# Attention output as 32-row products per head, small copies moved to ScalarE, another list order, and the flag read earlier

## The chip, the cores and the metric

The kernel runs on one core of a Trainium2 chip. A core has five engines that run their own instruction streams beside each other: TensorE (PE, the matmuls; PEld is its weight load), VectorE (DVE), ScalarE (ACT), GpSimd (POOL) and SyncE (SP, which here only issues DMAs). The metric is the device time of one execution in microseconds (us), lower is better.

## The reference, cut to what matters

Three stages follow each other. An attention of 4 batches and 8 heads over 32 memory slots, a mixture of 8 experts with the two best per token, and a second MLP.

```python
def _attn_ref(q, k, v, phi):          # (4, 8, 576, 64), phi (4, 8, 576, 32)
    a = softmax(phi, over the 32 slots)
    k_m = np.einsum('bhsm,bhsd->bhmd', a, k)
    v_m = np.einsum('bhsm,bhsd->bhmd', a, v)
    attn = softmax(scale * q @ k_m.T)  # 576 x 32 per head
    return attn @ v_m                  # 576 x 64 per head

def _moe_ref(x, w_gate, w_noise, noise, w1, w2):   # x (2304, 512), 8 experts, F = 1024
    logits = x @ w_gate
    noisy = logits + log1p(exp(x @ w_noise)) * noise
    # two largest per token, softmax over them, relu(x @ w1[e]) @ w2[e], weighted sum

def _moe2_ref(x, w_in, w_out):         # 512 -> 2048 -> 512
    h = x @ w_in
    return (h * clip(h + 3, 0, 6) / 6) @ w_out
```

## The kernel before, in words

The attention is cut into 8 groups of four heads (batch b, half gi: g = 2b + gi). Four heads of 32 slots fill the 128 partitions. A group goes through the stages of the lists below: `ld` loads phi, q, k and v (L521 and on, queue SP); `a1` (L537) takes the softmax of phi; `q` (L553) transposes q on PE; `a2` (L571) multiplies it with k and v (72 products of 32x32 weights by 128 columns, L581) into km, scales them into kd (L585, L586), takes the largest value us of the v part (L594), and makes the transposed kT (L600, L602) and, with the gate's weights, a 16-column piece for the router's logits (L606, L609); `b` (L618) makes scores and their softmax `at`; `c` (L646) multiplies `at` with vb. vb (128 x 272) holds the four heads' v as a block diagonal of 256 columns, made by POOL (L649) from kd and the mask mp (L613), and the 16 logit columns. The product (L665) is taken in three pieces, each evacuated from PSUM by ACT (L667); after the second half of a batch DVE adds the logits (L671) and SP stores x to DRAM (L673).

After two batches the router (`route`, L682) finds the two best experts of each token and writes lists of token numbers, the first ones (ids0, L800) for an early part of expert 0, the full ones (ids, L802) at the end. POOL gathers rows of x by such a list (L836), PE transposes them (L853), and ACT and DVE split them into two fp16 parts (L855, L857). An expert's layer 1 is L870 (ACT L877, L878, DVE L880 follow), its layer 2 is L920, with ACT's yt (L923) and SP's store (L925) behind it. Weights come in as fp32 `st` (L447) and are split by ACT (L414) and DVE (L416). The second MLP (`ffn`, L994) runs over 6 chunks of 384 rows; its layer 1 is L1007, then DVE L1012, ACT L1014 (hf), DVE L1015, ACT L1017 (hh), DVE L1018; its layer 2 is L1031, and ACT L1045 and SP L1054 bring the rows out. `combine` (L931) gathers the two experts' rows of a chunk (ya and yb, L938), scales them (L945) and adds them. Last comes a flag: if the lists overflowed, a slower path runs behind `tc.If`; every engine loads the flag (L1226) and branches (L1227).

The order of the work is not that of the code. Functions register operations with an engine, a duration and dependences; `Sched` (L91) then places them on the engines by due times, in several rounds backwards and forwards, and each engine's instructions are written out in that order. It is steered by tables: `ORDER` and `W0`, `EAT` say in which step a group's stage is registered, `RUSH` shifts due times by stage and group, `W0G` says behind which group's loads the first expert's weights come. The operations fall into two segments; the first holds the attention, the router and the early part of expert 0, the second all the rest. Buffers are counted by tag: three of `kv`, so a load of group g + 3 waits for PE's products of group g.

## Time and profile before

| | |
|---|---|
| median of three runs | 917.58 us (917.4 to 918.63) |
| profiled execution | 916.52 us |
| its span | 914.7 us |
| instructions in the span | 16312 |
| PE busy | 874.2 us, 96% |
| DVE busy | 617.7 us, 68% |
| ACT busy | 436.9 us, 48% |
| POOL busy | 139.4 us, 15% |

Busy time is the time in which an engine executes at least one instruction; waiting, register work and DMA issues do not count. A line such as L665 is the source line that issued an instruction; a name such as kd is a tile, and `out<-in` says what is written from what. Idle time is put down to what ended it, so the table of shares is only the start: the waits and the chain of work have to be read stretch by stretch.

### The profile page before, as it was taken

What the parts mean: (1) busy time and instruction counts of PE and PEld (TensorE: products, weight loads), DVE (VectorE), ACT (ScalarE), POOL (GpSimd) and SP (SyncE); (2) the same over time, 40 slices, a digit from 0 to 9 for tenths busy, and PEclk for the clock granted to TensorE, in tenths of its full rate; (3) what the DMA queues carried; (4) which work ended last, traced back from release to release, by engine and by line L of the source; (5) the groups of instructions that cost most, each with busy time, mean ns of one, the idle gap of its engine ahead of it and who ended that gap; (6) DMA issues with size and microseconds to landing.
All of it is one profiled execution on the core that took longest, in us unless ns stands there. A gap on an engine that the chain in (4) does not pass through costs nothing.

```text
span 914.7 us, 16312 instructions
## 1 busy us (share of the span) xinstructions
PE 874.2 (96%) x6612; PEld 516.0 (56%) x6612; DVE 617.7 (68%) x1088; ACT 436.9 (48%) x665; POOL 139.4 (15%) x155
## 2 busy tenths in 40 slices
PE   6798699989999999999999998999999999999996
PEld 6676475654747565665656554555555555555552
DVE  6798965868697958688789896876464543333432
ACT  2386426665756647474836645453332422322222
POOL 2234211312021111000002123432010000000000
PEclk8999699999999999999999999999999999999998
DMA  9955335859996767959776546451310301200101
GB/s 342 362 173 179 95 127 198 284 166 224 214 262 211 214 216 200 229 123 282 238 231 213 171 145 177 105 139 52 78 35 1 78 1 18 52 1 2 33 1 38
DMA packets 109537, 135.14 MB, mean 148 GB/s; under 512 B 53008, under 2 KB 74000, under 8 KB 109456
## 3 DMA queue, kind: packets, MB, share of 16 engines
q1 hardware_dynamic: 103312, 114.63, 41.8%
q0 software_dynamic: 6144, 19.40, 8.0%
q8 instruction: 54, 0.88, 0.4%
q14 instruction: 27, 0.22, 0.1%
HBM read 94.74 MB, written 27.86 MB: 134 GB/s over the span
## 4 chain that ended last, share of the span: by engine, by line
PE 76%; DMA 4%; DVE 4%; issue 2%; ACT 1%; POOL 0%; SPq 0%; POOLq 0%; DVEq 0%; ACTq 0%
PE o L1031 19%; PE two L1007 18%; PE two L870 18%; PE o L920 14%; PE o L897 3%; DMA xg<-xf,ids 2%; PE da L870 1%; DMA ya<-ys,slot 1%; PE oa L920 1%; DMA st<-wf 1%; DVE yt L906 0%; DVE wam L457 0%; DVE xT L857 0%; DVE hh L880 0%; DVE xg L966 0%
## 5 line engine op out<-in xcount | busy, mean ns | idle before, releaser
L1031 PE MATMUL o<-wb,hh 128*128 128x512 f16 x864 | 194.8, 379 | 3.1 <-ACT hh L1017 2.4
L1007 PE MATMUL two<-xT,wa 128*128 128x384 f16 x1152 | 195.7, 326 | 0.0
L1007 PEld LDWEIGHTS <-wa 128*128 128x128 f16 x1152 | 112.5, 98 | 79.6 <-DVE wsm L400 0.2
L1031 PEld LDWEIGHTS <-hh 128*128 128x128 f16 x864 | 84.0, 98 | 99.7 <-ACT hh L1017 2.8
L920 PEld LDWEIGHTS <-hh 128*128 128x128 f16 x720 | 69.6, 98 | 80.5 <-issue 3.0
L1014 ACT ACTIVATE hf<-hf,c 128x768 f32<-128x768 f32 x48 | 44.9, 935 | 145.5 <-DVE hf L1012 138.7
L1012 DVE TENSOR_TENSOR hf<-two,ivb 128x768 f32<-128x768 f32 x48 | 45.9, 956 | 93.9 <-PE two L1007 93.8
L870 PE MATMUL two<-xT,wb 128*128 128x304 f16 (+2 forms) x768 | 103.8, 295 | 2.9 <-ACT hh L878 2.9
L870 PEld LDWEIGHTS <-wb 128*128 128x128 f16 x768 | 75.8, 99 | 31.0 <-issue 3.1
L870 PEld LDWEIGHTS <-wa 128*128 128x128 f16 x768 | 75.7, 99 | 29.9 <-issue 2.0
L870 PE MATMUL two<-xT,wa 128*128 128x304 f16 (+1 forms) x672 | 90.3, 295 | 0.7 <-DVE war L431 0.4
L920 PE MATMUL o<-wb,hh 128*128 128x512 f16 x384 | 86.5, 379 | 0.0
L920 PE MATMUL o<-wa,hh 128*128 128x512 f16 x336 | 75.3, 379 | 0.0
L880 DVE TENSOR_TENSOR hh<-hf,hh 128x608 f16<-128x608 f32 (+2 forms) x72 | 49.3, 689 | 37.8 <-ACT hh L878 35.6
L836 POOL DMA_INDIRECT xg<-xf,ids x40 | 46.3, 1157 | 161.6 <-DVE ya L845 57.4
L877 ACT ACTIVATE hf<-two 128x608 f32<-128x608 f32 (+2 forms) x72 | 42.9, 595 | 54.0 <-PE two L870 51.2
L1015 DVE SCALAR_TENSOR_TENSOR hh<-hf,two 128x768 f32<-128x768 f32 x48 | 45.7, 951 | 31.8 <-ACT hf L1014 31.6
L1018 DVE TENSOR_TENSOR hh<-hh,hh 128x768 f16<-128x768 f32 x48 | 45.9, 957 | 29.5 <-ACT hh L1017 29.5
L1017 ACT ACTIVATE hh<-hh 128x768 f16<-128x768 f32 x48 | 40.4, 842 | 41.8 <-DVE hh L1015 41.8
L416 DVE SCALAR_TENSOR_TENSOR wb<-st,wsm,wb 128x1024 f16<-128x1024 f32 x40 | 50.5, 1280 | 4.1 <-ACT wb L414 3.8
L416 DVE SCALAR_TENSOR_TENSOR wa<-st,wsm,wa 128x1024 f16<-128x1024 f32 x40 | 51.4, 1310 | 1.7 <-ACT wa L414 0.9
L414 ACT ACTIVATE wa<-st,wsm 128x1024 f16<-128x1024 f32 x40 | 44.1, 1144 | 8.1 <-DVE wsm L402 8.1
(220 smaller groups left out, 1079.7 us busy)
## 6 DMA issues: line engine op xcount, KB each, us to landing
st<-moe_w_d SPq DMA_DIRECT2D x32, 1024.0 KB
ys<-yt SPq DMA_DIRECT2D x32, 256.0 KB
w<-moe_w_in_d SPq DMA_DIRECT2D x16, 512.0 KB
wf<-w64o SPq DMA_DIRECT2D x32, 256.0 KB
w<-moe_w_out_d SPq DMA_DIRECT2D x16, 512.0 KB
st<-wf SPq DMA_DIRECT2D x8, 1024.0 KB
kv<-k_d SPq DMA_DIRECT2D x8, 576.0 KB
kv<-v_d SPq DMA_DIRECT2D x8, 576.0 KB
```

The source lines that it names most:

```text
L414: sch.op("ACT", act(1024, ptr=1), lambda s=s, w=w, c=c: ACT.activation(w.t[:, 0, c], s.t[:, c], AF.Copy, scale=sm.t[:, 2]), [(s, i), (sm, ...
L416: sch.op("DVE", 1.28, lambda s=s, w=w, c=c: DVE.scalar_tensor_tensor(w.t[:, 1, c], s.t[:, c], sm.t[:, 2], w.t[:, 0, c], op0=ALU.mult, op1= ...
L836: sch.op("POOL", 1.05, lambda t=t, xg=xg, tw=tw: POOL.indirect_dma_start(out=xg.t[:tw], out_offset=None, in_=xf[:rows], in_offset=bass.Ind ...
L870: PE.matmul(ph.t[:, i, :nw], wa.t[:, wi, c * 1024 + fb * 128:c * 1024 + fb * 128 + 128], xT.t[:, 4 * xi + c, o0 + i * nw:o0 + (i + 1) * nw ...
L880: sch.op("DVE", dve(n), lambda: DVE.tensor_tensor(hh.t[:, 1], hf.t, hh.t[:, 0], op=ALU.subtract), [hf, (hh, 0)], [(hh, 1)])
L920: PE.matmul(py.t[:tw], hs[fb].t[:, hi, tsl], wb.t[:, wi, fb * 512:(fb + 1) * 512], start=(fb == 0 and n == 0), stop=(fb == 7 and n == 2))
L1007: PE.matmul(ph.t[:, i, :CW], win[fb // 8].t[:, wi, o:o + 128], xT.t[:, 4 * xi + kc, :CW], start=(n == 0), stop=(n == 11))
L1012: sch.op("DVE", dve(768), lambda: DVE.tensor_tensor(t1.t, ph.t[:, :, :CW], ivb.t[:, None, :CW].to_broadcast([128, 2, CW]), op=ALU.mult), [ ...
L1014: sch.op("ACT", act(768, ptr=1), lambda: ACT.activation(t1.t, t1.t, AF.Relu, bias=c3, scale=CG), [], [t1])
L1015: sch.op("DVE", dve(768), lambda: DVE.scalar_tensor_tensor(gf.t, t1.t, 6.0 * CG, ph.t[:, :, :CW], op0=ALU.min, op1=ALU.mult), [t1, ph], [gf])
L1018: sch.op("DVE", dve(768), lambda: DVE.tensor_tensor(g.t[:, 1], gf.t, g.t[:, 0], op=ALU.subtract), [gf, (g, 0)], [(g, 1)])
L1031: PE.matmul(po[m_].t, g.t[:, gi, i, m_ * 128:(m_ + 1) * 128], wou[fb // 8].t[:, wi, (fb % 8) * 512:(fb % 8 + 1) * 512], start=(fb == 0 and ...
```

## The change

Stage c's product now runs by heads: for each of six blocks of 96 rows, four products of 32 rows by 64 columns, head h on partitions 32h to 32h + 31, into two PSUM buffers, and six full products of 16 columns for the logits. vs, v by a power of two, is a copy by ACT; mp, maskp and POOL's vb are gone. ACT evacuates two pieces of 768 columns, and for a batch's first half the 96 logit columns; DVE adds the logits of the second half straight from PSUM, and x goes out in two stores per batch instead of three. In stage a2, ACT makes kd[0] and a new plain copy vv of scaled v, and us is the maximum over vv. The tables `ORDER`, `RUSH` and `W0G` and the planner's DMA rates have other values. The flag is computed in the slot of chunk 2 and loaded by every engine ahead of PE's first instruction of the last chunk; the branch stays at the end. The very last store, 96 rows, is issued by ACT.

```diff
-ORDER = (('ld', -1), ('b', 1), ('r', 6), ('q', 0), ('a1', -1), ('c', 3), ('a2', 0))
+ORDER = (('ld', -1), ('b', 1), ('a1', 0), ('r', 6), ('q', 0), ('c', 3), ('a2', 0))
-W0G = (4, 7)
+W0G = (2, 7)
...
         def f():
-            DVE.tensor_scalar(kd.t[:, 0], km.t[:, 0, None, :].to_broadcast([128, 2, D]), st.t[:, 2:3], None, op0=ALU.mult)
             DVE.scalar_tensor_tensor(kd.t[:, 1], km.t[:, 1, None, :].to_broadcast([128, 2, D]), st.t[:, 2:3],
                                      mask2, op0=ALU.mult, op1=ALU.mult)
...
+        sch.op("ACT", act(128, True, 1), lambda: ACT.activation(
+            kd.t[:, 0], km.t[:, 0, None, :].to_broadcast([128, 2, D]), AF.Copy, scale=st.t[:, 2:3]), [km, (st, 2)], [(kd, 0)])
+        vv = new("vv", [128, D])
+        sch.op("ACT", act(64, True, 1), lambda: ACT.activation(vv.t, km.t[:, 1], AF.Copy, scale=st.t[:, 2:3]),
+               [km, (st, 2)], [vv])
...
-            u.t[:, gi:gi + 1], kd.t[:, 1].rearrange("p a d -> p (a d)"), axis=AX.X, op=ALU.max,
-            apply_absolute_value=True), [kd], [(u, gi)])
+            u.t[:, gi:gi + 1], vv.t, axis=AX.X, op=ALU.max, apply_absolute_value=True), [vv], [(u, gi)])
...
-            mp = new("mp", [128, 256])
...
+        sm, vs = scales[b], new("vs", [128, D])
+        sch.op("ACT", act(64, False, 1), lambda: ACT.activation(vs.t, vv.t, AF.Copy, scale=sm.t[:, 2]), [vv, (sm, 2)], [vs])
...
+            for j, c in enumerate(cs):
+                for h in range(4):
+                    hs = slice(32 * h, 32 * h + 32)
+                    PE.matmul(po[h // 2].t[:PT, h % 2, j * D:(j + 1) * D], at.t[hs, c], vs.t[hs], start=True, stop=True)
+            for j, c in enumerate(cs):
+                PE.matmul(po[1].t[:PT, 0, 384 + 16 * j:400 + 16 * j], at.t[:, c], vg.t, start=True, stop=True)
+        sch.op("PE", 1.8, f, [at, vs, vg], po)
+        for i in range(2):
+            sch.op("ACT", act(768, True), lambda i=i: ACT.activation(
+                hl.t[:, :, gi, 128 * i:128 * i + 128].rearrange("p j (h d) -> p h j d", h=2),
+                po[i].t[:PT, :, :384].rearrange("p h (j d) -> p h j d", d=D), AF.Copy), [po[i]], [(hl, (gi, i))])
+        pl = lambda: po[1].t[:PT, 0, 384:480].rearrange("p (j e) -> p j e", e=16)
+        if gi == 0:
+            sch.op("ACT", act(96, True), lambda: ACT.activation(lg.t, pl(), AF.Copy), [po[1]], [lg])
+            return
+        L, c = Ls[b // 2], b % 2 * NJ
+        sch.op("DVE", dve(96), lambda: DVE.tensor_tensor(L.t[:, c:c + NJ], lg.t, pl(), op=ALU.add), [po[1], lg], [(L, c)])
...
+                last = c == NC2 - 1 and m_ == 2 and p0 > m_ * 128
+                dma(lambda rows=rows, pi=pi, n=n, ot=ot, o=o, last=last: (ACT if last else SP).dma_start(
+                    rows[pi:pi + n], ot.t[o:o + n]), n * 2048, [ot], eng="ACT" if last else "SP")
...
+                    if fv is None and o.eng == "PE" and o.n >= mark:
+                        assert flagged.issubset(seen)
+                        fv = nc.values_load(flag[0:1, 0:1], min_val=0, max_val=1,
+                                            skip_runtime_bounds_check_because="a comparison's result")
```

Three places show how rows stand on an engine. The numbers behind names only count buffers and differ between the two kernels. First DVE in group 3, from its kd on; here before the change (e is the transposed softmax of phi, sc the scores, us the maximum, war the scale search):

```order
L585 TENSOR_SCALAR kd_734<-oa_641,st_503 128x128
L586 SCALAR_TENSOR_TENSOR kd_734<-oa_641,st_503,mask_136 128x128
L575 STREAM_TRANSPOSE e_746<-aT_624 128x576
L594 TENSOR_REDUCE us_630<-kd_734 128x1
L627 STREAM_TRANSPOSE sc_759<-da_725 128x576
L424 TENSOR_REDUCE war_765<-us_630 128x1
L629 TENSOR_REDUCE sm_768<-sc_759 128x18
L428 TENSOR_SCALAR wdg_773<-identb,war_765 128x128
```

And after it, where line numbers are a few lower:

```order
L581 SCALAR_TENSOR_TENSOR kd_754<-oa_655,st_616,mask_136 128x128
L594 TENSOR_REDUCE us_625<-vv_758 128x1
L571 STREAM_TRANSPOSE e_775<-aT_653 128x576
L420 TENSOR_REDUCE war_812<-us_625 128x1
L537 STREAM_TRANSPOSE aT_814<-ph_348 128x576
L424 TENSOR_SCALAR wdg_817<-identb,war_812 128x128
L538 TENSOR_REDUCE st_819<-aT_814 128x1
```

The kd[0] row (L585) is gone, the maximum us reads vv, which ACT writes, and stands directly behind kd[1].

The second place is ACT at the seam between expert 7 and the second MLP: hf and hh belong to chunk 0 of the second MLP, wb is the weight split, yt expert 7's last output tile, ya the scaled rows for chunk 1. Before:

```order
L1014 ACTIVATE hf_6506<-hf_6506,c_134 128x768
L1017 ACTIVATE hh_6539<-hh_6528 128x768
L1014 ACTIVATE hf_6537<-hf_6537,c_134 128x768
L414 ACTIVATE wb_6571<-st_10_6504,wsm_6526 128x1024
L923 ACTIVATE yt_6573<-o_37_6393,iys 128x512
L414 ACTIVATE wb_6571<-st_10_6504,wsm_6526 128x1024
L1017 ACTIVATE hh_6593<-hh_6557 128x768
L1014 ACTIVATE hf_6591<-hf_6591,c_134 128x768
L414 ACTIVATE wb_6571<-st_10_6504,wsm_6526 128x1024 x2
L1017 ACTIVATE hh_6625<-hh_6613 128x768
L945 ACTIVATE ya_6611<-ya_6611,fac_178 96x512
```

After (L925 is yt, L1016 hf, L1019 hh, L410 wb, L947 ya):

```order
L925 ACTIVATE yt_6657<-o_37_6569,iys 128x512
L1016 ACTIVATE hf_6690<-hf_6690,c_134 128x768
L1019 ACTIVATE hh_6723<-hh_6716 128x768
L1016 ACTIVATE hf_6721<-hf_6721,c_134 128x768
L410 ACTIVATE wb_6760<-st_10_6694,wsm_6714 128x1024 x2
L1019 ACTIVATE hh_6787<-hh_6762 128x768
L1016 ACTIVATE hf_6766<-hf_6766,c_134 128x768
L410 ACTIVATE wb_6760<-st_10_6694,wsm_6714 128x1024
L947 ACTIVATE ya_6712<-ya_6712,fac_175 96x512
L947 ACTIVATE ya_6718<-ya_6718,fac_175 96x512
L1019 ACTIVATE hh_6816<-hh_6809 128x768
```

yt has moved from behind the second hf and one wb to ahead of the first hf; more of the ya scalings stand between one hh and the next.

The third place is the end of SP's list, with the output stores, the flag's load and the branch. Before:

```order
L1054 DMA out_d<-yt_9356 96x512
L1054 DMA out_d<-yt_9356 32x512
L1054 DMA out_d<-yt_9375 64x512 x2
L1054 DMA out_d<-yt_9382 32x512
L1054 DMA out_d<-yt_9382 96x512
L1226 TENSOR_LOAD flag
L1227 COMPARE_AND_BRANCH
```

After:

```order
L1233 TENSOR_LOAD flag
L1058 DMA out_d<-yt_9145 96x512
L1058 DMA out_d<-yt_9145 32x512
L1058 DMA out_d<-yt_9159 64x512 x2
L1058 DMA out_d<-yt_9184 96x512
L1058 DMA out_d<-yt_9184 32x512
L1058 DMA out_d<-yt_9540 96x512
L1058 DMA out_d<-yt_9540 32x512
L1058 DMA out_d<-yt_9559 64x512 x2
L1058 DMA out_d<-yt_9566 32x512
L1239 COMPARE_AND_BRANCH
```

The flag's load stands ahead of the stores of the last two chunks' six tiles, and the last 96-row store is no longer in SP's list; between the last store and the branch nothing is left.

## Rows read from the trace of the kernel before

**Rows 1.** Page: busy us, share, instructions; group's busy, mean ns, idle before it.
```profile
PE 874.2 (96%) x6612; PEld 516.0 (56%) x6612; DVE 617.7 (68%) x1088; ACT 436.9 (48%) x665; POOL 139.4 (15%) x155
...
L1031 PE MATMUL o<-wb,hh 128*128 128x512 f16 x864 | 194.8, 379 | 3.1 <-ACT hh L1017 2.4
```

**Rows 2.** Stretches: length, busy PE, PEld, DVE, ACT, POOL; clock, DMA share, GB/s.
```profile
0.00:30.00 30.00, 20.10 (x413) 17.47 (x417) 18.05 (x57) 7.50 (x14) 6.98 (x25) 0.89 0.91 329
50.00:70.00 20.00, 19.50 (x387) 15.05 (x382) 19.58 (x49) 16.35 (x29) 4.65 (x4) 1.00 0.47 150
70.00:104.40 34.40, 29.41 (x380) 21.31 (x370) 30.77 (x105) 19.10 (x40) 12.66 (x14) 0.93 0.53 167
104.40:142.00 37.60, 29.72 (x208) 20.46 (x209) 25.92 (x73) 13.83 (x28) 10.17 (x11) 0.84 0.36 114
142.00:914.70 772.70, 757.49 (x4829) 427.44 (x4827) 507.09 (x764) 370.08 (x535) 97.19 (x95) 0.99 0.48 136
```

**Rows 3.** Line L800: duration ns min/median/max, first and last start us.
```profile
L800 DVE TENSOR_SCALAR ids<-idf x1: 157/157/157, 104.4 to 104.4; 128x2 int32<-128x2 f32 x1
```

**Rows 4.** Chain that ended last, 85 to 145 us: start us, us, what.
```profile
113.40 5.51 PE da L870 x35
...
141.75 3.31 PE two L870 x21
```

**Rows 5.** Lines L585, L594, L613, L671 on DVE, columns as in rows 3.
```profile
L585 DVE TENSOR_SCALAR kd<-oa,st x8: 310/350/351, 15.9 to 81.5; 128x128 f32<-128x128 f32 x8
...
L594 DVE TENSOR_REDUCE us<-kd x8: 235/256/286, 17.1 to 83.9; 128x1 f32<-128x128 f32 x8
...
L613 DVE TENSOR_SCALAR mp<-maskp,wsm x4: 344/370/1100, 32.8 to 90.6; 128x256 f32<-128x256 f32 x4
...
L671 DVE TENSOR_TENSOR L<-hl x12: 145/176/643, 58.7 to 101.0; 96x32 f32<-96x32 f32 x12
```

**Rows 6.** Groups by form, 0 to 104.4 us: busy us, mean ns | idle before.
```profile
L667 ACT ACTIVATE hl<-da 96x544 f32<-96x544 f32 x24 | 14.4, 615 | 9.1 <-PE da L665 7.9 <-PE oa L747 1.2
...
L566 ACT ACTIVATE qT<-da 128x640 f32<-128x640 f32 x8 | 5.6, 701 | 17.2 <-PE da L564 17.0
...
L566 ACT ACTIVATE qT<-da 128x512 f32<-128x512 f32 x8 | 4.7, 593 | 1.7 <-PE da L564 1.7
```

**Rows 7.** Timeline, PE, 60 to 68 us: start us, us, instructions together.
```profile
59.82 2.03 PE L581 MATMUL oa<-kv,e 32*32 32x128 f32 x68
...
62.27 2.91 PE L665 MATMUL da<-vb,at 128*96 128x272 f32 x12
...
66.27 0.29 PE L606 MATMUL oa<-wgn,kT 128*64 128x16 f32 x4 [0.47 <-ACT kT L602]
```

**Rows 8.** Chain that ended last, 530 to 566 us.
```profile
538.79 0.68 ACT yt L923
...
549.56 7.41 DMA ya<-ys,slot
...
562.54 3.63 PE o L1031 x16
```

**Rows 9.** Timeline, PE, 525 to 535 us.
```profile
526.27 7.96 PE L1007 MATMUL two<-xT,wa 128*128 128x384 f16 x48
```

**Rows 10.** Timeline, SP, two stretches from 906.5 to 909.1 us.
```profile
905.99 1.21 SPq L1054 DMA_DIRECT2D out_d<-yt  x2
...
907.25 1.80 SPq L1054 DMA_DIRECT2D out_d<-yt  x1
```

**Rows 11.** Line L1226, the flag's loads, columns as in rows 3.
```profile
L1226 PEldq TENSOR_LOAD <-flag x1: 485/485/485, 902.0 to 902.0; - x1
...
L1226 SPq TENSOR_LOAD <-flag x1: 548/548/548, 909.1 to 909.1; - x1
```

**Rows 12.** Chain that ended last, 895 to 914.7 us.
```profile
894.78 11.24 PE o L1031 x52
...
906.10 0.69 ACT yt L1045
```

More of the change, by code (lines that the diff above doesn't have):

```diff
@@ L28 @@
 NE0 = 2
-XC = 272
 NFIRST = 1
@@ L592, in stage_a2 @@
         u = us[b]
-        pk, kT, vg, vb = new("oa", [128, 2, 128]), new("kT", [128, 2, 128]), new("oa", [128, 16]), new("vb", [128, XC])
-        sch.op("DVE", dve(128), lambda: DVE.tensor_reduce(
-            u.t[:, gi:gi + 1], kd.t[:, 1].rearrange("p a d -> p (a d)"), axis=AX.X, op=ALU.max,
-            apply_absolute_value=True), [kd], [(u, gi)])
+        pk, kT, pg, vg = new("oa", [128, 2, 128]), new("kT", [128, 2, 128]), new("oa", [128, 16]), new("vg", [128, 16])
+        sch.op("DVE", dve(64), lambda: DVE.tensor_reduce(
+            u.t[:, gi:gi + 1], vv.t, axis=AX.X, op=ALU.max, apply_absolute_value=True), [vv], [(u, gi)])
         def f():
@@ L654, in stage_c @@
         if gi == 0:
-            hls[b] = [new("hl", [PT, 2, 2, XC]) for _ in range(3)]
+            hls[b] = new("hl", [PT, NJ, 2, 256]), new("lg", [PT, NJ, 16])
         elif b % 2 == 0:
             Ls[b // 2] = new("L", [PT, 2 * NJ, 16])
-        rows = xf[b * S:(b + 1) * S, :].rearrange("(p j) (g c) -> p j g c", j=NJ, g=2)
-        for i in range(3):
-            po, hl = new("da", [PT, 2, 512]), hls[b][i]
-            def f(i=i, po=po):
-                for j in range(2):
-                    c = j * 288 + i * PT
-                    PE.matmul(po.t[:, j, :XC], at.t[:, c:c + PT], vb.t, start=True, stop=True)
-            sch.op("PE", 1.15, f, [at, vb], [po])
-            sch.op("ACT", act(2 * XC, True), lambda po=po, hl=hl: ACT.activation(hl.t[:, :, gi], po.t[:, :, :XC], AF.Copy),
-                   [po], [(hl, gi)])
-            if gi:
-                L, c = Ls[b // 2], b % 2 * NJ + 2 * i
-                sch.op("DVE", dve(32), lambda c=c, hl=hl, L=L: DVE.tensor_tensor(
-                    L.t[:, c:c + 2], hl.t[:, :, 0, 256:], hl.t[:, :, 1, 256:], op=ALU.add), [hl], [(L, c)])
-                dma(lambda i=i, hl=hl: SP.dma_start(rows[:, 2 * i:2 * i + 2], hl.t[:, :, :, :256]),
-                    393e3, [hl], [(xfk, (b, i))])
@@ new lines, in stage_c, with f @@
+        hl, lg = hls[b]
+        po = [new("da", [128, 2, 512]) for _ in range(2)]
+        def f():
+            cs = [slice(j % 2 * 288 + j // 2 * PT, j % 2 * 288 + (j // 2 + 1) * PT) for j in range(NJ)]
+            for j, c in enumerate(cs):
[4 more added lines that the diff above has]
+                PE.matmul(po[1].t[:PT, 0, 384 + 16 * j:400 + 16 * j], at.t[:, c], vg.t, start=True, stop=True)
@@ L677, in attn_moe_kernel @@
+        L, c = Ls[b // 2], b % 2 * NJ
+        sch.op("DVE", dve(96), lambda: DVE.tensor_tensor(L.t[:, c:c + NJ], lg.t, pl(), op=ALU.add), [po[1], lg], [(L, c)])
+        rows = xf[b * S:(b + 1) * S, :].rearrange("(p j) c -> p j c", j=NJ)
+        for i in range(2):
+            r = slice(3 * i, 3 * i + 3)
+            dma(lambda r=r: SP.dma_start(rows[:, r], hl.t[:, r].rearrange("p j g c -> p j (g c)")),
+                590e3, [hl], [(xfk, (b, i))], rate=350e3)
     sums = [sch.keep() for _ in range(B // 2)]
@@ L682, in route @@
     def route(b):
-        assert len(Ls[b].wr) == NJ
-        L, sms = Ls.pop(b), [scales.pop(2 * b + i)[0] for i in range(2)]
+        assert len(Ls[b].wr) == 2
+        L, sms = Ls.pop(b), [scales.pop(2 * b + i) for i in range(2)]
         bc = [PT, NR, NE]
@@ L1072, in early @@
     def early():
-        assert ids0k.wr and len(xfk.wr) >= 6
+        assert ids0k.wr and len(xfk.wr) >= 4
         xTe.append(new("xT", [128, 8, CAP], F16))
-        gather(0, 0, NE0, xTe[0], lambda t: ids0[:, t:t + 1], ids0k, [(xfk, (b, j)) for b in range(2) for j in range(3)], 2 * S)
+        gather(0, 0, NE0, xTe[0], lambda t: ids0[:, t:t + 1], ids0k, [(xfk, (b, j)) for b in range(2) for j in range(2)], 2 * S)
     def early1():
@@ L1196, in attn_moe_kernel, with f @@
     for c in range(NC2):
+        if c == NC2 - 1:
+            mark = len(sch.ops)
+        elif c == 2:
+            def f():
+                DVE.tensor_reduce(fl[:, 0:1], cnt[:, 1], axis=AX.X, op=ALU.max)
+                DVE.tensor_scalar(fl[:, 0:1], fl[:, 0:1], float(CAP), None, op0=ALU.subtract)
+                DVE.tensor_scalar(fl[:, 1:2], cnt[:, 0, NE - 1:NE], float(NFIRST * 128), None, op0=ALU.subtract)
+                DVE.tensor_reduce(fl[:, 0:1], fl, axis=AX.X, op=ALU.max)
+                DVE.tensor_scalar(flag, fl[:, 0:1], 0.5, None, op0=ALU.is_gt)
+            sch.op("DVE", 0.6, f, [cntk], [flagk])
         def mid(c=c):
```

55 lines of the change are left out of this document (18 added, 37 removed).

## The prediction, made before the changed kernel ran

> **What bounds the kernel now.** I read the busy shares first: TensorE (PE) works 96% of the span [rows 1], so the change can win only where PE waits. The table by stretches shows where that is: 9.9 of the first 30 us, 0.5 between 50 and 70, 5.0 up to 104.4, 7.9 up to 142, then 15.2 in the last 773 us [rows 2]. I then asked what ends the wait in each.
>
> In the attention it is VectorE (DVE): 19.58 of 20 us busy from 50 to 70 and 30.77 of 34.4 up to 104.4 [rows 2]. Its last product there is the first list of token numbers, at 104.4 [rows 3]; two gathers of x rows follow, PE transposes them, and early layer 1 of expert 0 starts at 113.40. The full list fetches the rest, and the main stream of experts starts at 141.75 [rows 4]. From there PE hardly stops, so what the lists come earlier by is about what the program ends earlier by. Two waits lie behind: at the seam between expert 7 and the second MLP, and after the last matmul; both are taken up below.
>
> **The change part by part: DVE.** The kd[0] copy leaves DVE (8 x 0.350 us), mp goes (4 x 0.370), the sum of logits L needs 4 instructions for 12 (12 x 0.176 gone), and the maximum us runs over 64 elements, not 128 (8 x 0.256 gone): 2.80 + 1.48 + 2.11 + 2.05 = 8.44 us [rows 5]. Back come 8 maxima over 64, between half of 0.256 and all of it; I take 0.20, so 1.6 us. And 4 sums of 96 columns, between 0.176 (32 columns) and 0.370 (256) [rows 5]; I take 0.25, so 1.0 us. Net 5.8 us. Some 1.6 of it (three groups' copies and maxima, one mp) falls in the first 30 us, where DVE is busy only 18.05 [rows 2] and may not pass it on: 4.2 to 5.8.
>
> Against this stands a new wait. The maximum us read DVE's own kd before; now it reads vv, which ScalarE (ACT) writes after kd[0]. In group 3 it stands directly behind kd[1] on DVE, and behind it are the transpose e, which PE needs for the next group's products, and the scale search. With ACT free, two small copies of some 0.25 us (worked out below) end 0.15 us after DVE's own 0.35: 8 x 0.15 = 1.2 us. With ACT inside an evacuation it is up to 1 us each, 8 us in all. ACT is busy 16.35 of 20 us from 50 to 70 [rows 2]; but the last four groups have 2 to 7 other DVE instructions in between, so I take 1.3. The front gains 5.8 - 1.3 = **4.5 us**.
>
> **ACT.** Twenty-four evacuations of 0.615 us (14.8 us) become 16 of 768 columns, 4 of 96, and 24 small copies. From 512 columns at 0.593 and 640 at 0.701 [rows 6] a column costs 0.84 ns and the start 0.16 us, so 768 take 0.81, 128 take 0.27, 96 take 0.24, 64 take 0.21: 16 x 0.81 + 4 x 0.24 + 8 x 0.27 + 16 x 0.21 = 19.4 us, 4.6 more. From 50 to 104.4 ACT works 35.5 of 54.4 us [rows 2], which leaves room: cost 0, except in the wait above. POOL's eight products vb only leave.
>
> **PE.** Twelve instructions of 272 columns took 2.91 us, 0.243 each [rows 7]. Now there are 48 of 64 columns, in four row parts, and 12 of 16 columns. The 32x32 products, which also take four parts of the array by turns, went at 2.03/68 = 0.030 us each, and those of 16 columns at 0.29/4 = 0.073 [rows 7]. I take 48 x 0.030 + 12 x 0.073 = 2.3 us a group, 0.6 less; if all 60 cost 0.073, 4.4 us, 1.5 more. Since DVE ends this stage, I put the 0.6 at nothing.
> The Trainium skill, "TensorEngine Tiling (Array Packing)", section Instruction Overhead, speaks against such cutting: a matmul has an overhead of some 60 cycles, so that few columns cost as much as 60. By that rule alone 60 instructions would take an estimated 1.5 us a group at 2.4 GHz. The 16-column rows stand well above it (0.073 us, not 0.025), so the rows decide; by the rule the stage would be shorter still, and the sum the same.
>
> **Loads.** Expert 0's first weights, 2.1 MB in two loads, move on SP from behind group 4's q to ahead of group 3's k and v. At 329 GB/s [rows 2] they delay those by 6.4 us and relieve later groups by as much. I put it at 0, with 6.4 us either way as bounds. The stores of x become 8 of 576 KB instead of 12 of 384, the same bytes; the first gather waits for four of them rather than six: 0.
>
> **Seam.** Chunk 0 of the second MLP waits 3.1 us on PE, 2.4 of it for ACT's hh [rows 1]. The chain: expert 7's last yt runs on ACT at 538.79, its store and then chunk 1's gathers follow, and one of these, issued at 549.56, lands 7.41 us later; ACT stands in the scaling of its rows with hf queued behind, and PE resumes at 562.54 [rows 8]. In the new order the last layer-2 products of expert 7 come ahead of all of chunk 0 on PE, and yt comes ahead of the first hf on ACT, not behind the second and a weight split. Chunk 0's first hf needs 24 products (48 take 7.96 us [rows 9]) and DVE's multiplication; from chunk 0's start (526.27) the new yt is due at about 528, some 10 us earlier. Six scalings of ya, not three, stand before the fourth hf; three more pairs of gathers at 0.9 us or more use up 5 of the 10. Gain **3.0 us**; if gathers are late again, 0.
>
> **Tail.** SP issues the last stores, the very last for 1.80 us from 907.25 [rows 10], and only then loads the flag, at 909.1 for 0.548 us [rows 11]; the span ends at 914.7. In the new order SP loads the flag a chunk earlier, and ACT issues the last 96 rows. SP is through with the store before the last at 907.20 [rows 10], so its branch can come then instead of at 909.65: 2.45 us. ACT ends its scaling at 906.79 [rows 12] and issues its 96 rows in 0.6 us (two took 1.21) to 1.80 [rows 10], so it branches between 907.4 and 908.6: the gain lies between 1.0 and 2.2; I take 2.2, as most issues are short. The flag load takes 0.485 us in PE's queue, and before it was there at 902.0 [rows 11], 4 us ahead of the end of the last matmul (906.02 [rows 12]): the queue runs ahead of the array, so I put it at 0, at most 0.5.
>
> **Sum.** 4.5 + 3.0 + 2.2 = 9.7 us off the profiled run of 916.5 (span 914.7 and 1.8 around it): 906.8. The median of the runs is 1.1 above that run, so 907.9.
>
> **Rivals.**
> *ACT takes DVE's place.* us and the kT chain wait behind evacuations of 0.81 us that were 0.615, and the front gains nothing: 917.6 - 5.2 = 912.4; with the full 8 us of waits the front loses 2.2, 914.6; a little more is no change. For it: ACT's 82% from 50 to 70. Against: the 35% that ACT is idle up to 104.4.
> *The seam keeps its wait,* because six scalings stand in front of the fourth hf: 910.9. Against it: yt's 10 us.
> *Row parts do not run side by side* (the slower side). The 60 loads and products of a group go one after another at 0.073 to 0.11 us (the 0.073 of a 16-column one, and half as much again for 64 columns), 4.4 to 6.6 us, +1.5 to +3.7. From 50 to 104.4 PE has only 5.5 us idle [rows 2]; eight groups at +2.5 are 20 us, 14.5 past that slack. With the 5.2 behind, 917.6 + 9.3 = 926.9. It eats into the time from +0.7 us a group, and the program is slower from about +1.6. Against it: the 0.030 us of the 32x32 products.
> *The tail does not shorten,* as the end hangs on the last store's landing and not on SP's branch: 910.1.
>
> **How the numbers follow.** Forecast 57%, ACT in DVE's place 20%, seam kept 11%, row parts in series 8%, tail kept 4%. The forecast's own range is 904 to 911. Downwards, no new wait and the weights' move worth most of its 6.4 us give 902; upwards I go to 914.5, ACT's full waits. A difference under 0.2% (1.8 us) is what a measurement of this kernel can't tell from none: a quarter of the ACT case (5%) ends there. Slower is the series case, 8%; faster the rest, 87%.
>
> **What would show it.** In the new profile: a group's 60 instructions in 2.0 to 2.6 us; the first list near 100 and the main stream near 137; DVE's us waiting for ACT under 0.3 us each; no wait for hh at the seam; SP's branch right behind the 32-row store. Wrong it is if the lists come no earlier than 103, if ACT's vv ends more than 4 us of DVE's waits, or if PE in the attention is busier than before.

## The result, and the profile after

The changed kernel is slower. Its median is 930.34 us of 4 runs (924.8 to 933.97) against 917.49 us of the kernel before in the same runs (916.06 to 918.63), ratio 1.0115 with a 95% interval of 1.0084 to 1.0147. A second set of runs gave 1.0102 (1.0081 to 1.0123). The forecast was 907.9 us, the range 902 to 914.5. The profiled execution took 930.74 us, its span is 928.9 us: 14.2 us more than before.

The page after, as in [rows 1]: busy us, share, instructions, then groups with their busy time, mean ns and the idle time before them.

```profile
PE 882.4 (95%) x6996; PEld 530.5 (57%) x6996; DVE 613.4 (66%) x1068; ACT 442.5 (48%) x685; POOL 136.3 (15%) x142
...
L1009 PE MATMUL two<-xT,wa 128*128 128x384 f16 x1152 | 195.6, 326 | 0.6 <-DVE wsm L396 0.6
L1033 PE MATMUL o<-wb,hh 128*128 128x512 f16 x864 | 194.9, 379 | 0.2
...
L872 PE MATMUL two<-xT,wb 128*128 128x304 f16 (+2 forms) x768 | 101.8, 293 | 1.6 <-ACT hh L880 1.6
...
L872 PE MATMUL two<-xT,wa 128*128 128x304 f16 (+1 forms) x672 | 92.0, 299 | 2.8 <-ACT hh L880 2.3
L922 PE MATMUL o<-wb,hh 128*128 128x512 f16 x384 | 86.2, 379 | 1.4 <-ACT yt L925 1.4
```

The seam's wait is gone: L1033 (L1031 before) has 0.2 us of idle time ahead of it, not 3.1 [rows 1]. But the expert layers now wait 1.6 + 2.8 + 1.4 us, where the page before had 2.9 + 0.7 + 0, so by these rows PE waits as long as before in the main stream, only elsewhere. VectorE (DVE) did lose work, 4.3 us of it (617.7 to 613.4).

The stretches, with the columns of [rows 2], and the line that writes the first list, as in [rows 3]:

```profile
0.00:30.00 30.00, 20.69 (x405) 18.00 (x409) 15.82 (x53) 9.57 (x20) 4.88 (x19) 0.89 0.96 357
30.00:50.00 20.00, 15.62 (x345) 13.76 (x338) 12.54 (x31) 9.97 (x23) 4.59 (x4) 0.83 0.65 238
50.00:70.00 20.00, 19.11 (x496) 16.24 (x492) 16.02 (x44) 11.65 (x25) 4.59 (x4) 1.00 0.66 230
70.00:112.40 42.40, 38.69 (x746) 34.46 (x741) 35.72 (x109) 26.16 (x55) 10.18 (x10) 0.74 0.32 108
```
```profile
L802 DVE TENSOR_SCALAR ids<-idf x1: 165/165/165, 112.4 to 112.4; 128x2 int32<-128x2 f32 x1
```

The second of these stretches in the kernel before, which [rows 2] does not show:

```profile
30.00:50.00 20.00, 17.99 (x423) 14.29 (x419) 16.31 (x45) 10.04 (x20) 7.75 (x9) 1.00 0.92 360
```

Between 50 and 70 us DVE is busy 16.02 us of 20, no longer 19.58 [rows 2], and the attention is not faster for it: the first list comes at 112.4 us, 8.0 later. PE is still busy 19.11 of 20. That is the first sign of what went wrong: the engine that was relieved was not the one that set the pace. ScalarE (ACT) has 11.65 us there where it had 16.35, so by its busy time it did not take DVE's place either. Between 30 and 50 us PE is busy 2.4 us less than before: there it waits more.

Where the time goes is read from PE's timeline (start us, us, instructions together, idle time and what ended it), first three rows of before, then those after:

```profile
29.25 2.80 PE L581 MATMUL oa<-kv,e 32*32 32x128 f32 x90 [0.25 <-DVE vb L609]
32.51 1.72 PE L581 MATMUL oa<-kv,e 32*32 32x128 f32 x54 [0.46 <-issue]
...
37.34 4.13 PE L581 MATMUL oa<-kv,e 32*32 32x128 f32 x144
```
```profile
29.47 2.80 PE L577 MATMUL oa<-kv,e 32*32 32x128 f32 x90
34.97 2.75 PE L577 MATMUL oa<-kv,e 32*32 32x128 f32 x54 [2.69 <-issue]
...
41.35 0.29 PE L605 MATMUL oa<-wgn,kT 128*64 128x16 f32 x4 [1.69 <-ACT kT L601]
...
42.22 5.80 PE L577 MATMUL oa<-kv,e 32*32 32x128 f32 x144
...
49.36 1.38 PE L658 MATMUL da<-vs,at 32*96 32x64 f32 x48
50.67 1.19 PE L660 MATMUL da<-vg,at 128*96 128x16 f32 x12
...
73.25 5.66 PE L577 MATMUL oa<-kv,e 32*32 32x128 f32 x144 [0.62 <-DVE vg L608]
...
92.73 2.66 PE L658 MATMUL da<-vs,at 32*96 32x64 f32 x48
95.32 2.10 PE L660 MATMUL da<-vg,at 128*96 128x16 f32 x12
```

Group 2's products (L577) halt in their middle for 2.69 us, and no semaphore ends the halt; before they halted 0.46 us there. Group 3's start at 42.22 instead of 37.34: 4.9 us are lost by then. The halt is most likely a wait for code. The page after counts the packets, megabytes and share of a DMA queue that carries instructions:

```profile
q8 instruction: 57, 0.93, 0.4%
```

That is 16 KB a packet, one for some 123 of PE's 6996 products. In both kernels the halts come at the same places of PE's program: at 25.2 and 32.5 us before, at 25.5 and 35.0 after, each time 126 products apart. The trace's record of single packets shows one of this queue ending 1.3 to 1.5 us ahead of each of these resumptions. In all 18 profiles there are 62 such halts from 18 to 112 us; they stand at a few places, multiples of some 127 products apart, and each ends 1.2 to 1.6 us behind such a packet. For the halt in group 2 it ends at 31.2 before, and only at 33.7 after, where it starts at 32.6, when PE has already stopped. What delays the packet no run shows.

Stage c's new product is nearly as short as forecast, 1.38 + 1.19 = 2.57 us in group 0 and up to 1.61 + 1.19 in group 4 at the higher clock level, against 2.91 [rows 7]; but the same instructions take 2.66 + 2.10 in group 5. And 144 small products take 5.80 and 5.66 us in groups 3 and 6, but 4.13 in group 7. The next table says why: its third column from the end is the granted clock.

```profile
73.00:76.20 3.20, 2.95 (x56) 2.61 (x60) 3.13 (x11) 2.88 (x6) 1.53 (x2) 0.51 0.00 0
...
94.00:104.00 10.00, 9.07 (x122) 8.56 (x118) 8.68 (x39) 6.74 (x13) 3.35 (x5) 0.50 0.56 181
```

0.50 is 1.2 GHz of 2.4. In the kernel before the attention runs at 1.00 from 20 to 92 us, and the clock falls behind a wait of 2.9 us at 89:

```profile
91.83 4.68 PE L665 MATMUL da<-vb,at 128*96 128x272 f32 x12 [2.91 <-POOL vb L649]
```
```profile
92.00:96.00 4.00, 4.00 (x11) 2.59 (x11) 3.96 (x18) 1.34 (x3) 1.76 (x2) 0.58 0.31 88
```

In the changed kernel it falls at 35.5, behind the halt, at 42.3, at 73.0, and at 93.5, the last time although PE was busy for 20.13 of the 20.25 us ahead: what it ran were the 16- and 64-column products of stage c, scores and small transposes. This is one execution. A second profile of the same kernel (span 928.7 us) has group 3's products at the higher level, and there the last of these falls comes at 96.5, behind a wait for ACT's vs:

```profile
41.96 4.13 PE L577 MATMUL oa<-kv,e 32*32 32x128 f32 x144
...
96.91 2.19 PE L658 MATMUL da<-vs,at 32*96 32x64 f32 x48 [2.46 <-ACT vs L645]
```

Its first list comes at 111.6, 0.8 us earlier than in the first profile.

After the list the difference grows again, from 8.0 us to 13.7 at the start of early layer 1 proper (127.09, before 113.40 [rows 4]); main stream 155.84, before 141.75: +14.1. The timeline of that place, all engines:

```profile
112.40 0.17 DVE L802 TENSOR_SCALAR ids<-idf 128x2 int32<-128x2 f32 x1
...
112.88 1.30 POOL L838 DMA_INDIRECT xg<-xf,ids  x1 [11.12 <-DVE ids L802]
112.93 0.79 SPq L675 DMA_DIRECT2D xf<-hl  x2
...
114.47 1.99 POOL L838 DMA_INDIRECT xg<-xf,ids  x1 [0.30 <-issue]
...
121.32 1.94 PE L855 MATMUL oa<-ident,xg 128*128 128x128 f32 x8 [9.19 <-DMA xg<-xf,ids]
```

The last batch's two stores of x, 576 KB each, are issued 0.05 us after the first gather, and the gathered rows reach PE 8.4 us after it; before, the stores had gone by then, and it was 3.8 us (list at 104.36, gather at 104.83, first transpose at 108.61).

The end, as in [rows 10 to 12]: timeline, and the flag's load.

```profile
909.45 12.47 PE L1033 MATMUL o<-wb,hh 128*128 128x512 f16 x57
...
918.13 5.72 SPq L1058 DMA_DIRECT2D out_d<-yt  x5
...
922.72 0.40 ACTq L1058 DMA_DIRECT2D out_d<-yt  x1
```
```profile
L1233 SPq TENSOR_LOAD <-flag x1: 534/534/534, 803.8 to 803.8; - x1
```

The last matmul ends at 921.92, the span 6.98 us later; before 8.68 (906.02 to 914.7). SP's last issue ends at 923.85, 5.05 us ahead of the end, as the flag's load did before (909.65 to 914.7). That fits the forecast, that SP's branch ends the program; no run shows the branch apart from the last store's landing. Other profiles of these kernels and their variants have 4.8 to 5.7 us there, and from the last matmul to the end 7.5 and 8.2 us with the old end and 6.5 to 8.0 with the new, so less than the 1.7 of these two may be gained.

### The profile page after: what moved, and what is told of

The parts are those of the page before. It is cut to its first block, busy times and chain, and to the rows that moved or that the text cites. A ratio compares the mean times of both kernels' runs of the same rounds, so it can differ in the third digit from the quotient of the medians.

```text
span 928.9 us, 17052 instructions
## 1 busy us (share of the span) xinstructions
PE 882.4 (95%) x6996; PEld 530.5 (57%) x6996; DVE 613.4 (66%) x1068; ACT 442.5 (48%) x685; POOL 136.3 (15%) x142
## 5 line engine op out<-in xcount | busy, mean ns | idle before, releaser
L1033 PE MATMUL o<-wb,hh 128*128 128x512 f16 x864 | 194.9, 379 | 0.2
L1033 PEld LDWEIGHTS <-hh 128*128 128x128 f16 x864 | 84.1, 98 | 96.5 <-DVE hh L1020 0.6
L1016 ACT ACTIVATE hf<-hf,c 128x768 f32<-128x768 f32 x48 | 44.9, 935 | 149.0 <-DVE hf L1014 141.8
L872 PE MATMUL two<-xT,wb 128*128 128x304 f16 (+2 forms) x768 | 101.8, 293 | 1.6 <-ACT hh L880 1.6
L838 POOL DMA_INDIRECT xg<-xf,ids x40 | 52.3, 1308 | 166.2 <-DVE ya L847 74.4
L1019 ACT ACTIVATE hh<-hh 128x768 f16<-128x768 f32 x48 | 40.4, 842 | 43.4 <-DVE hh L1017 41.6
L410 ACT ACTIVATE wa<-st,wsm 128x1024 f16<-128x1024 f32 x40 | 44.5, 1145 | 12.1 <-DVE wsm L398 12.1
```

What stands on the lines that cost most here:

```text
L410: sch.op("ACT", act(1024, ptr=1), lambda s=s, w=w, c=c: ACT.activation(w.t[:, 0, c], s.t[:, c], AF.Copy, scale=sm.t[:, 2]), [(s, i), (sm, ...
L838: sch.op("POOL", 1.05, lambda t=t, xg=xg, tw=tw: POOL.indirect_dma_start(out=xg.t[:tw], out_offset=None, in_=xf[:rows], in_offset=bass.Ind ...
L872: PE.matmul(ph.t[:, i, :nw], wa.t[:, wi, c * 1024 + fb * 128:c * 1024 + fb * 128 + 128], xT.t[:, 4 * xi + c, o0 + i * nw:o0 + (i + 1) * nw ...
L1016: sch.op("ACT", act(768, ptr=1), lambda: ACT.activation(t1.t, t1.t, AF.Relu, bias=c3, scale=CG), [], [t1])
L1033: PE.matmul(po[m_].t, g.t[:, gi, i, m_ * 128:(m_ + 1) * 128], wou[fb // 8].t[:, wi, (fb % 8) * 512:(fb % 8 + 1) * 512], start=(fb == 0 and ...
```

## Experiments

Two theories stood at the beginning. T-tables: the new order lists, the early weights above all, cost the time. T-clock: the short products let the clock fall, and that costs it. Ratios are to the kernel before in the same set of runs; a kernel's own runs vary by up to 12 us here (932.08 to 944.38 in one case), so differences under 0.4% between two kernels decide nothing.

**The lists apart from the operations.** The changed kernel with the old tables (RUSH and the rates of the group's loads go back as well):

```diff
-ORDER = (('ld', -1), ('b', 1), ('a1', 0), ('r', 6), ('q', 0), ('c', 3), ('a2', 0))
+ORDER = (('ld', -1), ('b', 1), ('r', 6), ('q', 0), ('a1', -1), ('c', 3), ('a2', 0))
...
-W0G = (2, 7)
+W0G = (4, 7)
...
-    def dma(fn, nbytes, r=(), w=(), nom=None, rate=330e3, eng="SP"):
+    def dma(fn, nbytes, r=(), w=(), nom=None, rate=300e3, eng="SP"):
```


> The changed kernel with the order table, the rush times, the place of the first weights and the planner's DMA rates all as before. Theory T-tables (the new order lists cost the time, the first weights ahead of group 3's loads above all): group 3's products start near 37 us again, the first list comes at 104 or earlier, and with seam and tail gained the time is 905 to 914 us. Rival T-clock (the short products of stage c let TensorE's clock fall while it is busy): the clock still falls from about 90 us on, the first list comes at 106 to 112 and the time stays at 922 to 932 us.

Measured: 938.36 us, 1.0217 (1.0186 to 1.0248); first list at 111.28, main stream at 159.67. T-tables falls in its simple form: with the old lists the new operations are slower still, and slower than either forecast. Then the groups of the early weights alone:

```diff
-W0G = (2, 7)
+W0G = (4, 7)
```


> The changed kernel with only the place of the first weights as before (behind group 4's loads). If the weights' place alone is the cause: group 3's products at about 37.5 us instead of 42.2, the first list 5 to 8 us earlier, 922 to 926 us. If it is the other tables or the clock: at most 2 us better than the changed kernel, 928 to 931 us.

Measured: 932.86 us, 1.0155 (1.0127 to 1.0183). Group 3 starts at 36.8, the list comes at 108.69, 3.7 us earlier, the main stream at 152.15; yet the whole is no better. Group 2's products run in one piece here, without the halt. The other way round, the old operations in the new lists (of the kernel before, only the tables and rates are edited):

```diff
-ORDER = (('ld', -1), ('b', 1), ('r', 6), ('q', 0), ('a1', -1), ('c', 3), ('a2', 0))
+ORDER = (('ld', -1), ('b', 1), ('a1', 0), ('r', 6), ('q', 0), ('c', 3), ('a2', 0))
...
-W0G = (4, 7)
+W0G = (2, 7)
```

> The kernel before with only the new tables and DMA rates. T-tables: slower than before by most of what the change lost and more, since the seam's gain alone is on the other side: 922 to 932 us, group 3's products near 42 us. T-clock: the long products of stage c keep the clock, so 914 to 919 us.

Measured: 937.29 us, 1.0191 (1.0149 to 1.0233); list at 109.43, main stream at 154.13. This kernel has the long products, and it is slower than either forecast: T-clock falls in its simple form too. Its clock falls all the same, at 38.4 us after waits of under 1 us, and group 3's products take 5.80 us. Each set of lists fits its own operations only: either mix is 2% slower than the kernel before, and moving one number of a table (W0G) moves everything behind it.

**The end alone.** The kernel before with the flag's early load and the last store on ACT:

```diff
-                dma(lambda rows=rows, pi=pi, n=n, ot=ot, o=o: SP.dma_start(rows[pi:pi + n], ot.t[o:o + n]),
-                    n * 2048, [ot])
+                last = c == NC2 - 1 and m_ == 2 and p0 > m_ * 128
+                dma(lambda rows=rows, pi=pi, n=n, ot=ot, o=o, last=last: (ACT if last else SP).dma_start(
+                    rows[pi:pi + n], ot.t[o:o + n]), n * 2048, [ot], eng="ACT" if last else "SP")
...
+                    if fv is None and o.eng == "PE" and o.n >= mark:
...
+                        fv = nc.values_load(flag[0:1, 0:1], min_val=0, max_val=1,
```

> The kernel before with only the flag's early load and the last store issued by ACT. Both theories: the attention is untouched, the span after the last matmul shortens from 8.7 to about 7.0 us, so 915.8 us, 1.7 less; 917.5 if the branch was not what ended the program.

Measured: 919.4 against 919.99 us, 0.9987 (0.9966 to 1.0007): 1.2 us less by the ratio, not told from nothing here. In its profile the end comes 7.9 us behind the last matmul, not the 7.0 expected.

**Fillers behind stage c.** A filler is a product that nothing reads; it only keeps PE busy. The planner's order is kept in all kernels from here on; only what is named differs from the changed kernel or, where that is said, from the kernel before. The kernel below has 20 fillers in the last three groups; a second one has 16 in all groups.

```diff
+            for _ in range(20 if g >= 5 else 0):
+                PE.matmul(po[1].t[:PT, 1, 384:], onesh[:, :PT], onesh, start=True, stop=True)
```


> The changed kernel, its order unchanged, with 20 extra products of 128 columns behind stage c's of the last three groups; they write a part of PSUM that nothing reads. T-clock: the granted clock, which fell to its lower level at 93.8 us in the changed kernel while TensorE was busy, falls later or less, and the list comes 1 to 4 us earlier in spite of 3 x 1.1 us more work on TensorE: 926 to 930 us where the changed kernel has 930.3. If the clock has nothing to do with it: the added work alone, 2 to 3.5 us later, 932 to 934 us.

> The changed kernel, its order unchanged, with 16 extra products of 128 columns behind stage c's in all eight groups (some 0.9 us each, 7 us in all). T-clock: no fall of the clock between 50 and 100 us, the three falls of the changed kernel's attention gone there, 925 to 930 us. Rival, TensorE's work sets the cadence of the groups and its clock does not matter: 5 to 7 us slower, 935 to 938 us.

Measured: 1.0167 (1.0131 to 1.0204) and 1.0179 (1.0162 to 1.0196), with the changed kernel itself at 1.0102 in the same set. The second loses what T-clock's rival said, some 7 us, although its clock stands at 1.00 from 90 to 100 us, where the changed kernel's is at 0.68. The first loses 6 to 7 us for 3.3 of added work, twice what its rival said; its runs lie 12 us apart, and the surplus stays open. Added work on PE in the attention comes out at the end, and a clock held by it did not pay for it.

> The changed kernel itself, for the comparison on one chip: ratio 1.0115 to before within its interval of 1.008 to 1.015.

**ACT's small copies given back to DVE:**

```diff
-        sch.op("ACT", act(128, True, 1), lambda: ACT.activation(
-            kd.t[:, 0], km.t[:, 0, None, :].to_broadcast([128, 2, D]), AF.Copy, scale=st.t[:, 2:3]), [km, (st, 2)], [(kd, 0)])
+        sch.op("ACT", act(128, True, 1), lambda: DVE.tensor_scalar(
+            kd.t[:, 0], km.t[:, 0, None, :].to_broadcast([128, 2, D]), st.t[:, 2:3], None, op0=ALU.mult), [km, (st, 2)], [(kd, 0)])
...
-        sch.op("ACT", act(64, True, 1), lambda: ACT.activation(vv.t, km.t[:, 1], AF.Copy, scale=st.t[:, 2:3]),
+        sch.op("ACT", act(64, True, 1), lambda: DVE.tensor_scalar(vv.t, km.t[:, 1], st.t[:, 2:3], None, op0=ALU.mult),
```

> The changed kernel, its order unchanged, but kd[0] and vv are written by VectorE at their places in the order, not by ScalarE. If the wait for ScalarE (kd[0], vv, then the transposes and kT) lengthens each group's chain: 3 to 8 us faster, 922 to 927 us. If VectorE's busy time still bounds the attention: 8 x 0.5 us slower, 933 to 935 us. T-clock or T-tables alone: within 2 us of the changed kernel.

Measured: 1.0148 (1.0104 to 1.0193), against 1.0102 for the changed kernel: no better. The interval is 4 us to either side, so a loss by DVE's 4 us more can't be excluded by it; in the profile the list comes at 109.9, not later than the changed kernel's 112.4 and 111.6. Neither ACT's place in the chain nor DVE's 4 us shows as what counts.

**The stores behind the gathers, the weights behind group 3, and both.**

```diff
-            dma(lambda r=r: SP.dma_start(rows[:, r], hl.t[:, r].rearrange("p j g c -> p j (g c)")),
-                590e3, [hl], [(xfk, (b, i))], rate=350e3)
+            o = dma(lambda r=r: (POOL if b == 3 else SP).dma_start(
+                rows[:, r], hl.t[:, r].rearrange("p j g c -> p j (g c)")), 590e3, [hl], [(xfk, (b, i))], rate=350e3)
+            if b == 3:
+                late_xf.append(o)
...
     order = sch.order()
+    order = [o for o in order if o not in late_xf]
+    i = max(order.index(o) for o in first_g) + 1
+    order[i:i] = late_xf
```

Here first_g holds the first two gathers. The second kernel, with ACT's first two reductions of these weights moved back too:

```diff
     order = sch.order()
+    order = [o for o in order if o not in w0_loads[0]]
+    i = max(order.index(o) for o in g_loads[3]) + 1
+    order[i:i] = w0_loads[0]
```

> The changed kernel in its order, but the last batch's two stores of x (576 KB each), which SP issued at 112.9 us beside the first gathers, are issued by GpSimd right behind those two gathers. Theory T-collision (the large stores hold the gathers up): the rows of the first gathers reach TensorE 3 to 4.5 us earlier than the 8.4 us after their issue, early layer 1 and the second list come as much earlier, 925 to 927.5 us. Rival, the gathers are late for another reason (their rows' own stores, the gather's engine): within 1 us of the changed kernel's 930.4.

> The changed kernel in its order, but expert 0's first weights are loaded behind group 3's loads, and ScalarE's first two reductions of them stand with the other two. Theory T-loads (the weights ahead of group 3 delay all later groups): group 3's products start at 37 to 38.5 us instead of 42.1 and the list comes 3 to 5 us earlier, 925 to 928 us. Rival, the delay is made good later by DVE's idle time: within 1.5 us of 930.4.

> Both edits together. If the two delays add up in the chain: 920 to 923 us, early layer 1 at 117 to 119 us instead of 127. If one hides the other: as the better of the two alone. If neither is the cause: 929 to 931 us.

With the stores moved (927.31 us, 1.0096, 1.0069 to 1.0123):

```profile
112.28 1.30 POOL L842 DMA_INDIRECT xg<-xf,ids  x1 [11.32 <-DVE ids L806]
113.88 1.99 POOL L842 DMA_INDIRECT xg<-xf,ids  x1 [0.30 <-DVE gt L701]
115.86 1.14 POOL L677 DMA_DIRECT2D xf<-hl  x2
116.08 1.08 PE L859 MATMUL oa<-ident,xg 128*128 128x128 f32 x4 [4.55 <-DMA xg<-xf,ids]
...
121.86 1.44 PE L876 MATMUL da<-xT,wa 128*128 128x256 f16 x6 [1.18 <-DVE xT L863]
```

The rows reach PE 3.8 us after the first gather's issue, as in the kernel before, early layer 1 starts at 121.86 and not at 127.09, the main stream at 150.69 and not at 155.84. That the large stores held the gathers up is shown: issued later, and by POOL in place of SP, they no longer do. In the profiles the main stream comes 5.2 us earlier, 0.6 of that with the list itself, so some 4.6 us of its delay of 14 are the stores'; in the whole time, by the ratios alone, the gain doesn't stand out from the scatter of the runs. The weights alone bring nothing: 1.0162 (1.0114 to 1.021), group 3 at 40.3, the list at 112.99. Both together: 922.44 us, 1.0038 (1.0024 to 1.0052), main stream at 150.22. That is clearly better than either, while its front is that of the stores alone; where the second part comes from stays open.

**Is it PE that sets the attention's pace?** The kernel before, with products that nothing reads behind each group's last piece of stage c:

```diff
+                for _ in range(16 if i == 2 else 0):
+                    PE.matmul(po.t[:, 1, 384:], onesh[:, :PT], onesh, start=True, stop=True)
```


> The kernel before in its order, with 16 extra products of 128 columns (some 0.9 us, written where nothing reads) behind each group's last piece of stage c, 7 us of TensorE's time in all. The prediction's premise (VectorE ends the attention, TensorE has slack): under 1.5 us slower. Rival (TensorE's own work and chain set the cadence of 10 us a group): 4 to 7 us slower.

Measured: 926.72 against 919.16 us, 1.0073 (1.0049 to 1.0097), 6.7 us by the ratio. One filler, two stretches with DVE's busy time third, and the first list:

```profile
67.64 1.06 PE L667 MATMUL da<-onesh 128*96 128x128 f16 x16
```
```profile
50.00:70.00 20.00, 19.11 (x367) 15.29 (x359) 17.26 (x42) 15.34 (x27) 3.47 (x3) 1.00 0.45 150
70.00:110.20 40.20, 35.73 (x550) 28.09 (x534) 33.65 (x114) 20.52 (x44) 13.06 (x14) 0.98 0.46 143
```
```profile
L802 DVE TENSOR_SCALAR ids<-idf x1: 157/157/157, 110.2 to 110.2; 128x2 int32<-128x2 f32 x1
```

Eight fillers of 1.06 us, 8.5 in all, put the list 5.85 us back (110.2 for 104.36) and the program 6.7. DVE, with the same work, falls from 19.58 to 17.26 us of 20. So PE has next to no slack there: the premise of the prediction is wrong, and DVE's high share was that of an engine kept at PE's pace. The counterpart, added work on DVE in the kernel before, was not run.

**Does the clock cost time at the end of the attention?** Fillers are now put only where PE waits: ahead of group 6's stage c (36 in the kernel before with the new end, 30 in the changed one with both edits) and of the first transposes of gathered rows.

```diff
+            for _ in range(30 if g == 6 else 0):
+                PE.matmul(po[1].t[:PT, 1, 384:], onesh[:, :PT], onesh, start=True, stop=True)
...
-            def f(xg=xg, px=px, tw=tw):
+            def f(xg=xg, px=px, tw=tw, warm=40 if (t0, nt, t) == (0, NE0, 0) else 0):
+                for _ in range(warm):
+                    PE.matmul(px.t[:, 0], onesh, onesh, start=True, stop=True)
```

> The kernel before with the new end (flag early, last store by ScalarE), and with products that nothing reads put where TensorE waits: 36 ahead of group 6's stage c, 40 ahead of the first transposes of gathered rows. T-clock (a low granted clock at the end of the attention costs time there): no fall at 92 us, the early layer 1 at the full clock from its start, 2 to 4 us faster than the end alone, 914 to 916 us. Rival (the second list, that is VectorE, ends this stretch, the clock is hidden): within 1 us of 918.

> The changed kernel in its order with the stores behind the gathers, the weights behind group 3, and products that nothing reads in TensorE's waits, 30 ahead of group 6's stage c and 40 ahead of the first transposes of gathered rows. T-clock: the clock stays up through stage c of groups 6 and 7 (4.3 us each at the lower level, 2.6 at the higher), 3 to 5 us faster than without, 917 to 919.5 us. Rival (clock hidden): 921 to 924 us.

Two more kernels have both edits and the small copies on DVE, by the diff above, without these fillers and with them:

> The changed kernel in its order with the stores behind the gathers, the weights behind group 3, and kd[0] and vv written by VectorE. If ScalarE's part in each group's chain is what is left of the loss: 917 to 920 us, level with before. If not: 921 to 924 us, as with the first two edits alone (922.4).

> All of these edits together. If ScalarE's place and the clock each hold a part: 914 to 917 us, faster than before. If neither: 921 to 924 us.

In the kernel before (with the new end) the clock now holds:

```profile
92.00:96.00 4.00, 2.99 (x12) 2.00 (x13) 3.96 (x18) 1.84 (x4) 2.35 (x3) 1.00 0.37 108
96.00:100.00 4.00, 3.11 (x26) 2.42 (x26) 3.97 (x19) 0.73 (x2) 1.04 (x3) 1.00 0.05 9
```

and so it does in the changed kernel up to 101, but not beyond:

```profile
93.00:97.00 4.00, 4.00 (x90) 3.35 (x89) 4.00 (x11) 4.00 (x10) 0.96 (x2) 1.00 1.04 411
97.00:101.00 4.00, 3.26 (x83) 3.04 (x82) 4.00 (x21) 3.11 (x7) 1.23 (x2) 1.00 0.11 38
101.00:105.00 4.00, 1.72 (x27) 1.51 (x26) 3.93 (x17) 1.96 (x5) 1.85 (x3) 0.73 0.94 278
```

Measured: before with fillers 0.9974 (0.9954 to 0.9994), list at 104.95 and main stream at 142.76, the list no earlier than with the end alone, the main stream 0.7 us earlier (104.89 and 143.42 there). Its clock falls again at 104.3 and 111.1, so the start of the early layer 1 was not tested at the higher level. The changed kernel with both edits and fillers 1.0052 (1.0023 to 1.0081), with both edits and the copies on DVE 1.0062 (1.003 to 1.0094), with all 1.0047 (1.0019 to 1.0074): none better than both edits alone. The 36 fillers cost nothing, so PE has slack there; and in these rows DVE is busy nearly the whole of 92 to 100 us in both kernels. So it is likely, though a high share alone does not show it, that from group 6's stage c on the lists wait for DVE and the clock is hidden behind it. Earlier, where PE sets the pace, no run here held the clock for nothing, so there its price stands only on the traces.

Of all kernels, before with the new end and fillers in the waits is the only one whose interval lies below 1, by 0.26%, which is not told from the end alone (0.9987); it is 1.3 to 1.4% faster than the changed kernel by the ratios.

## Why the prediction was wrong

The step that failed is "Since DVE ends this stage, I put the 0.6 at nothing", and with it "The front gains 5.8 - 1.3". I took DVE's 19.58 of 20 us for the bound and passed over the column beside it, PE's 19.50 of 20, although the prediction itself puts PE's wait there at 0.5 us. In the next 15 us PE is busy throughout, and DVE is not:

```profile
70.00:85.00 15.00, 15.00 (x289) 11.56 (x287) 12.16 (x32) 10.44 (x23) 7.58 (x7) 1.00 0.66 221
```

The sum per group says the same: 4.13 for the 32x32 products, 1.4 for q, 2.9 for stage c and 1.6 for the rest make about 10 us, the spacing of the groups in the kernel before (37.34, 47.80, 57.72, 67.89). Adding work to PE settled it: 8.5 us of products that nothing reads put the list 5.85 us back. The front lost 13.7 us where 4.5 were to be gained. The other terms that failed are the two that the prediction put at 0, loads and stores, below.

Point by point:
- *DVE's work* fell by 4.3 us (5.8 forecast). It bought nothing, as PE set the pace up to some 89 us.
- *The wait for ACT* came one instruction earlier than forecast: not at the maximum us (L594 has no idle time before it) but at kd[1]. Who DVE waited for from 37 to 112 us (us, times, longest):

```profile
DVE kd L581 <- ACT kd L584: 6.0, 3, 4.7
...
DVE kd L581 <- ACT vv L587: 1.8, 1, 1.8
```

Most of this idle time is a wait for PE's products, behind which ACT's copy takes its 0.37 us; but kd[0] on ACT and kd[1] on DVE, two halves of one tile, run at the same time in none of the eight groups, so the move of kd[0] did not shorten the chain. It is not what cost the time: with both copies back on DVE no kernel was better (1.0148 for 1.0102, 1.0062 for 1.0038). So the ACT rival, 20%, is not borne out either.
- *Stage c's product* takes 2.57 to 2.80 us at the higher level where 2.3 were forecast, as a 16-column product takes 0.099 us and not 0.073; the row parts do run side by side (48 in 1.38 us). The rival that they don't is refuted, although its side, slower, came: that its 926.9 us is nearer to the result than the forecast is luck.
- *"Loads ... I put it at 0, with 6.4 us either way"*: group 3 was 4.9 us late. But the weights' move explains at most 2 of it: with the weights back they come at 40.3 instead of 42.2, 1.0 of that by a higher clock, and the list gains nothing. The rows show where it was lost: 2.2 us more in the halt in group 2's products, 1.6 by the lower clock in the rest of them and in the q transposes, 0.5 in the wait for kT, and 0.65 for the scores' product that stands ahead of group 3's in the new list.
- *"The stores of x become 8 of 576 KB ... 0"* failed outright: the bytes are the same, but two stores land on the gathers, 4.6 us.
- *The seam* gained as forecast (3.1 to 0.2 us of waiting), and the new list gave as much away in the expert layers: the main stream to the last matmul takes 766.1 us, 764.3 before. Other profiles have 762 to 774 us with the new order of the main stream and 767 to 768 with the old, so neither a gain nor a loss stands out there.
- *The end* gained 1.7 us of 2.2 in these two profiles, and 1.2 (-0.6 to 3.1) by the runs with the end alone.

The ledger, changed kernel against before, from the two traces: group 3's products +4.9 us; end of group 3's stage c +6.8 (82.82, before 75.98); first list +8.0; early layer 1 +13.7; main stream +14.1; last matmul +15.9; end +14.2. From the first to the second, 5.80 and 5.66 for 4.13 us of the same products at the lower clock make 3.2 us, against 0.1 to 0.3 us saved in each stage c. In the second profile, where group 3's products take 4.13, group 4's start 1.9 us earlier, and 0.8 of that is left at the list. From the second to the third, stage c of groups 5 to 7 at the lower clock takes 4.3 to 4.8 us, not 2.6, ahead of the list's last products; holding the clock there brought nothing, so what those 1.2 us are made of is open. From the third to the fourth, 5.7 us, the stores make 4.6; the rest, 1.0, stands between the first transposes and early layer 1 and stays with the stores moved.

Open is what delays the code packet behind group 2's halt of 2.69 us (moving the weights in an order otherwise kept left it as it was), and why the clock falls at 42 and 73 us after waits under 1.7 us, when in the kernel before it outlasts 2.07 us at 23. The short products alone are not the reason: with the long ones the clock falls after short waits too, in the new lists at 38.4 us, and at 25.8 after 1.73 us in the kernel before with fillers, whose code up to there is that of the kernel before. With both edits the changed kernel is still 0.4% slower than the kernel before, and what that is made of is open too.
